# Reordering the passage from the first to the second token group in a fused attention and Fourier-mix kernel

## The chip, the cores and the metric

The kernel runs on one core of a Trainium2 chip. A core has a matrix engine (TensorE, PE in the profile, with its weight loads as PEld), a vector engine (VectorE, DVE), a scalar engine (ScalarE, ACT), a general engine (GpSimd, POOL), a queue engine (SyncE, SP) that issues most transfers, and 16 DMA engines. The metric is the device time in microseconds of one execution; lower is better.

## The reference

Inputs `q`, `k`, `v` have shape (8, 8, 576, 64): batch, heads, tokens, head size. Attention runs within chunks of 64 tokens. Its output, seen as (8, 576, 512), goes through a Fourier mixing block with a two-layer network:

```python
scores = scale * np.matmul(q_c, k_c.transpose(0, 1, 2, 4, 3))   # per chunk of 64
attn = softmax(scores); x = attn @ v_c                          # -> (8, 576, 512)
mixed = np.real(np.fft.fft(np.fft.fft(x, axis=1), axis=2))
u = x + mixed
un = (u - mean(u)) / np.sqrt(var(u) + 1e-6)
out = u + np.maximum(un @ w_ch1, 0.0) @ w_ch2                   # (512, 2048), (2048, 512)
```

The two weights arrive as 64-bit floats and are turned into 32-bit ones in the kernel. All arithmetic is float32.

## The kernel before

Tokens are handled in nine groups of up to 512: one for each of the eight batches and one for the tokens left over at the middle of each sequence. For a group, the two products of the network (first weight `w1` in `wa`, "up"; second weight `w2` in `wb`, "down") are the main loop, and everything else is fed in between: the loop `for _ in mlp(g)` counts steps `t` and after each step emits a share of the attention and the Fourier transform of the next batch (`sides`), of the rounding of the weights (`round_next`), and of stores. Each engine executes its instructions in the order in which they were emitted, so this order is the schedule.

Group 0 uses the plain products: `up_first` takes steps 1 to 16 and `down_plain` steps 17 to 32, one for each of 16 blocks `m` of the second weight, with four matmuls a step. Its four PSUM banks `dn` are freed by the output additions of L1249. From group 1 on a scheme of seven smaller products in place of eight is used (`up_halves`, `down_halves`). It needs sums of weight blocks and sums of token blocks:

- `keep1(pair)` forms the sums of the first weight for one of four pairs of blocks, four GpSimd additions (L1069), the results going into the front of `wb` and back into `wa`. `keep1_store(i)` writes the seven blocks of each pair to DRAM (`s1`): three of them are raw quarters of the weight, `a11`, `a12` and `a22` (numbers 0, 4 and 6), and four are sums (2, 1, 3, 5). Group 1 reads the blocks where they are; later groups read them from DRAM.
- `keep2(i)` forms those of the second weight, four GpSimd additions (L1087) with their stores (L1091) for each of four blocks. `keep2_whole` stores its raw blocks. `conv2` is the list of `keep2` steps; three of them are emitted in each step once all weights are rounded.
- `combined(g, q)` forms the token sums of one half of a group (L1024, L1025, L1026 on VectorE), and with `late` the last of them (L1022).

The passage from group 0 to group 1 runs so. The side work of batch 1 ends with its Fourier transform: products `z`, copies into `zr` and `zf` on ScalarE, and three products `mix` (L838), each followed by a ScalarE copy `y` (L843), two VectorE additions (L848, L849), additions to the tiles (L855, on VectorE for the low tile and GpSimd for the high one), and statistics (L702, L703, and L706, L707 on ScalarE). `normed` makes the normalised tile `un` (L992), `turned` transposes it on TensorE (L397) and copies it into `unT` (L1007). When the four tiles of group 1 are turned and the token sums made, `up_halves(1)` starts with the product `pb` of L1289, which reads the second result of `keep1(0)`. The attention of batch 2 begins in the same steps: scores L448 from `qT` and `kT`, which VectorE transposes (L416), softmax, and the value product L498. For a low tile the first token column of `qT` is copied to the end position, on GpSimd (L418, L431) or on ScalarE (L429).

Transposes, mixes and value products share two PSUM buffers of `ps_t`. `sizes[cur]` is the number of side steps of a batch, and `ready_at` the step by which they are to be done; `due` spreads them evenly. The core's SP queue takes the loads of `q`, `k` (L250), `v` (L273) and of the raw weights (L346), the stores of the outputs (L1037, L1046), of `s1` (L1074) and `s2` (L1091, L1099), and the loads of stored blocks (L1155, L1160), in the order of emission.

Of the kernel before, what the change touches and what calls it, by code (L numbers as in the profile page):

```python
# [16 lines left out]
def kernel(  # L17
# [43 lines left out]
    KF = DFF // 128  # L61
# [5 lines left out]
    G = 2 * NM  # L67
# [35 lines left out]
    NO, HF = 7, KF // 2  # L103
# [77 lines left out]
    NG = len(groups)  # L181
# [219 lines left out]
    def att_T(n, which="qk"):  # L401

        if n > first[2]:
            for src, dst, nm in ((qs, qT, "qT"), (ks, kT, "kT")):
                if nm[0] not in which:
                    continue
                a = src.pop(n).rearrange("p j (t b d) -> p j t b d", t=4, b=2)[:, :, :, 0]  # L410
                t = one_p.tile([128, NJ, 2, CH + 1], FP32, tag=nm, name=nm)
                low = kind(n) == LO and nm == "qT"
                to = t[:, :, :, CH:0:-1] if low else t[:, :, :, 0:CH]
                if kind(n) == HI:
                    to = to[:, :, ::-1]
                nc.vector.transpose(out=to.rearrange("p j c (r t) -> p j t c r", t=4), in_=a)  # L416
                if low:
                    nc.gpsimd.tensor_copy(t[:, :, :, 0:1], t[:, :, :, CH:CH + 1])  # L418
                dst[n] = t.rearrange("p j c t -> p (j c) t")
            if n + 1 < NT:  # L420
                load(n + 1, which)
            return
        a = qs.pop(n)
        pt = turn(lambda j: a[:, 2 * j:2 * j + 2, :].rearrange("p h d -> p (h d)"))
        t = one_p.tile([128, 2 * NJ, CH + 1], FP32, tag="qT", name="qT")
        low = kind(n) == LO
        nc.scalar.copy(t[:, :, CH:0:-1] if low else t[:, :, 0:CH], pt.rearrange("p j (c t) -> p (j c) t", c=2))
        if low and n < first[1]:
            nc.scalar.copy(t[:, :, 0:1], t[:, :, CH:CH + 1])  # L429
        elif low:  # L430
            nc.gpsimd.tensor_copy(t[:, :, 0:1], t[:, :, CH:CH + 1])  # L431
        qT[n] = t
        a2 = ks.pop(n)
        pt = turn(lambda j: a2[:, 2 * j:2 * j + 2, :].rearrange("p h d -> p (h d)"))
        t = one_p.tile([128, NJ, 128], FP32, tag="kT", name="kT")
        nc.scalar.copy(t, pt)
        kT[n] = t.rearrange("p j (c t) -> p (j c) t", c=2)
        if first[1] <= n + 1 < NT:
            load(n + 1)
# [530 lines left out]
        yield  # L970


    uns, unTs = {}, {}

    def natural(n):

# [38 lines left out]
    def combined(g, q_, late=False):  # L1015

        unT = unTs[g]
        cl, ch = slice(q_ * 128, (q_ + 1) * 128), slice(256 + q_ * 128, 256 + (q_ + 1) * 128)
        b11, b12, b21, b22 = unT[:, 0:2, cl], unT[:, 0:2, ch], unT[:, 2:4, cl], unT[:, 2:4, ch]
        t1, t2, t4 = (tt_1[o][:, :, cl] if g == 1 else tt[:, o, :, cl] for o in range(3))  # L1020
        if late:
            nc.vector.tensor_tensor(out=t4, in0=b21, in1=t2, op=ALU.subtract)  # L1022
            return
        nc.vector.tensor_tensor(out=t1, in0=b12, in1=b11, op=ALU.subtract)  # L1024
        nc.vector.tensor_tensor(out=t2, in0=b22, in1=t1, op=ALU.subtract)  # L1025
        nc.vector.tensor_tensor(out=b12, in0=b22, in1=b12, op=ALU.subtract)  # L1026
        if g > 1:
            nc.vector.tensor_tensor(out=t4, in0=b21, in1=t2, op=ALU.subtract)
# [39 lines left out]
        ):  # L1068
            nc.gpsimd.tensor_tensor(out=out_, in0=in0, in1=in1, op=op)  # L1069

    def keep1_store(i):
        pair, o = i // NO, (2, 1, 5, 3, 0, 4, 6)[i % NO]
        to = s1[pair, o].rearrange("p (k x) -> p k x", k=2)
        nc.sync.dma_start(out=to, in_=parts1(pair)[o])  # L1074

# [153 lines left out]
    def down_plain(g, h1):  # L1229

        dns = [ps_f.tile([128, 512], FP32, tag="ff", name="dn") for _ in groups[g]]
        for m in range(KF):
            for s, dn in enumerate(dns):
                nc.tensor.matmul(  # L1236
                    out=dn,
                    lhsT=h1[:, m, s * 128:(s + 1) * 128],
                    rhs=w2[:, m, :],
                    start=(m == 0),  # L1240
                    stop=(m == KF - 1),
                )
                if m == KF - 1:
                    n = groups[g][s]
                    if s < G - 1:
                        o = three_p.tile([128, DM], FP32, tag="o", name="o")
                    else:
                        o = one_p.tile([128, 2 * (HM + 1)], FP32, tag="two", name="o")[:, 0:DM]
                    nc.vector.tensor_tensor(out=o, in0=dn, in1=natural(n), op=ALU.add)  # L1249
                    store(n, o)  # L1250
            for j in range(G):
                due = KF - (G - j + 1)
                if m == due - 2:
                    normed(g + 1, j)
                if m == due:
                    turned(g + 1, j)
                    if j >= 2 and g + 1 >= first_of[1]:
                        combined(g + 1, j - 2)
            yield


# [175 lines left out]
    with tc.manual_schedule():  # L1437
# [60 lines left out]
        begin = [0]  # L1498
        for g in range(NG):
            begin.append(begin[-1] + (KF if g < first_of[1] else 2 * HF) + (KF if g < first_of[2] else 2 * NO if g < FEW else NR2 // 2))  # L1500
        ready_at = [begin[g] + (2 * KF - 7 if g < first_of[2] else 2 * HF + 4) for g in range(NG)]
        conv2 = iter([step for i in range(HF // 2) for step in [keep2(i ^ 1)]])

        def chain(gens):
            for gen in gens:
# [5 lines left out]
        for g in range(NG):  # L1511
            for _ in mlp(g):
# [7 lines left out]
                if cur < len(sides):  # L1520
                    t0 = 3 if cur == 0 else ready_at[cur - 1]
                    t1 = ready_at[cur]
                    due = min(sizes[cur], (t - t0) * sizes[cur] // (t1 - t0))
                    while done < due:
                        heavy = next(sides[cur], None) or heavy
                        done += 1
                    if t >= t1:
                        for _ in sides[cur]:
                            pass
                        cur, done = cur + 1, 0  # L1530
                if not heavy:
                    round_next(late if t < KF and t % 4 == 3 else None)
                    if t <= 2 or t < KF and t % 4 == 0 or t >= KF + 3:
                        round_next()
# [7 lines left out]
                if t == begin[1] - 1:  # L1542
                    for _ in conv2:
                        pass
                if begin[1] - 1 <= t < begin[1] + 7 and t % 2:
                    keep1((t - begin[1] + 1) // 2)
                if t == ready_at[NG - 3]:
                    rest_ = make_rest()
# [6 lines left out]
                    slab3.extend(a.rearrange("p (m e) -> p m e", m=4) for a in more)  # L1555
                if begin[FEW] + 2 <= t < begin[FEW] + 2 + NS3:
                    fetch(3)
                if begin[1] < t < begin[1] + KF:
                    for i in range(2):
                        if n_kept < HF // 2 * NO:  # L1560
                            keep1_store(n_kept)
                            n_kept += 1
                if t in (begin[1] + 9, begin[1] + 13, begin[1] + 16):
                    fetch(2)
                if t == begin[1] + KF:
# [51 lines left out]
```

## Time and profile before

| | |
|---|---|
| median of 3 runs | 1074.06 us (1072.5 to 1075.39) |
| profiled execution, its own time | 1074.23 us |
| its span in the profile | 1072.2 us |
| TensorE busy | 1046.3 us, 98% |
| VectorE busy | 610.8 us, 57% |
| GpSimd busy | 406.6 us, 38% |
| ScalarE busy | 315.3 us, 29% |
| moved by DMA | 212.74 MB, 198 GB/s on average |

Busy times are sums of the recorded instructions of one engine. The profile's own time is that of the span and what lies around it. In a timeline a row gives start, duration, engine, line, operation, the tile written and the tiles read, how many records are merged, and in brackets the idle time just before and what ended it. One float32 matmul of the program shows as two records.

### The profile page before, as it was taken

The page shows a single profiled execution, that of the slowest core. Times are in us where ns is not written, and L with a number is a line of the kernel's source. Part 1 is how long each engine was busy: PE and PEld are TensorE (multiplying, and loading weights), DVE is VectorE, ACT ScalarE, POOL GpSimd, SP SyncE. Part 2 cuts the span into 40 slices and gives each one's busy share as a digit, 9 for nine tenths or more (in the row PEclk, how much of TensorE's full clock was granted, in tenths as well). Part 3 has the DMA queues.
Part 4 walks back from the last instruction along what each step waited for, and adds up shares of the span by engine and source line. Part 5 has one row for each costly group of instructions (what it writes and reads, how often), then busy time and mean ns, then how long its engine had stood idle before and what let it go on. Part 6 is the DMA issues. An engine that isn't in the chain of part 4 may idle for free.

```text
span 1072.2 us, 20212 instructions
## 1 busy us (share of the span) xinstructions
PE 1046.3 (98%) x7498; PEld 854.6 (80%) x7498; DVE 610.8 (57%) x1319; ACT 315.3 (29%) x746; POOL 406.6 (38%) x531
## 2 busy tenths in 40 slices
PE   8999989899999999999999999999999999999997
PEld 6645444688888888888888888788888888888886
DVE  4798986684567465664565554745664535433331
ACT  4688563233113411322032312331133103101200
POOL 4310018672415140344134321614161726780281
PEclk9999999999999999999999999999999999999999
DMA  8767565489668546883667266954654559776763
GB/s 176 232 186 218 123 196 189 139 249 312 233 199 232 149 140 198 239 232 119 191 209 231 99 182 195 231 165 163 202 177 116 208 191 350 229 231 199 272 228 106
DMA packets 157759, 212.74 MB, mean 198 GB/s; under 512 B 69308, under 2 KB 103100, under 8 KB 151390
## 3 DMA queue, kind: packets, MB, share of 16 engines
q1 hardware_dynamic: 154012, 208.04, 63.4%
q10 hardware_dynamic: 3330, 2.76, 1.1%
q8 instruction: 60, 0.98, 0.4%
q0 software_dynamic: 320, 0.66, 0.3%
q14 instruction: 37, 0.30, 0.1%
HBM read 177.31 MB, written 34.08 MB: 197 GB/s over the span
## 4 chain that ended last, share of the span: by engine, by line
PE 77%; DVE 8%; DMA 5%; ACT 4%; SPq 3%; issue 2%; POOL 1%; DVEq 0%; ACTq 0%; POOLq 0%
PE pa L1289 19%; PE pb L1341 18%; PE pb L1289 14%; PE pa L1341 13%; PE dn L1405 4%; PE pt L397 2%; PE mix L838 2%; DMA xall<-in_moe_w_ch_dram 1%; SPq L263 1%; PE xp L498 1%; PE z L719 1%; DVE power L378 1%; DMA out_dram<-o 1%; PE sc L448 1%; DMA v<-in_v_dram 1%
## 5 line engine op out<-in xcount | busy, mean ns | idle before, releaser
L1289 PE MATMUL pa<-unT,wa 128*128 128x256 f32 x736 | 175.0, 381 | 2.5 <-DVE wa L1297 2.5
L1289 PEld LDWEIGHTS pa<-unT,wa 128*128 128x128 f32 x736 | 138.3, 190 | 21.8 <-DVE wa L1297 2.7
L1289 PE MATMUL pb<-wa 128*128 128x256 f32 x448 | 106.9, 381 | 0.1
L1341 PE MATMUL pa<-wb,h 128*128 128x256 f32 x448 | 101.5, 380 | 0.0
L1341 PE MATMUL pb<-wb,h 128*128 128x256 f32 x448 | 100.7, 379 | 0.0
L1289 PEld LDWEIGHTS pb<-wa 128*128 128x128 f32 x448 | 84.1, 190 | 12.3 <-DVE h L1299 0.5
L1341 PEld LDWEIGHTS pa<-wb,h 128*128 128x128 f32 x448 | 83.9, 190 | 11.3
L1341 PEld LDWEIGHTS pb<-wb,h 128*128 128x128 f32 x448 | 84.1, 190 | 11.0
L1169 POOL TENSOR_TENSOR h<-h 128x256 f32<-128x256 f32 x56 | 47.7, 860 | 102.3 <-DVE wb L1167 98.2
L555 POOL COPY xall<-xall 1x512 f32<-1x512 f32 x28 | 17.8, 636 | 154.3 <-DVE xall L515 126.9
L1295 DVE TENSOR_TENSOR wa<-pb,wa 128x256 f32<-128x256 f32 x56 | 23.8, 425 | 69.7 <-ACT wa L1294 69.7
L1289 PE MATMUL pb<-unT,wa 128*128 128x256 f32 x256 | 60.5, 379 | 0.0
L1303 ACT ACTIVATE h<-pa 128x256 f32<-128x256 f32 x64 | 24.6, 384 | 114.1 <-PE pa L1289 113.6
L1236 PE MATMUL dn<-wb,h 128*128 128x512 f32 x128 | 57.5, 597 | 0.0
L1294 ACT COPY wa<-pa 128x256 f32<-128x256 f32 x56 | 20.9, 372 | 123.5 <-PE pa L1289 80.6
L1289 PEld LDWEIGHTS pb<-unT,wa 128*128 128x128 f32 x256 | 48.6, 190 | 6.6
L1289 PE MATMUL pa<-wa 128*128 128x256 f32 x224 | 53.9, 383 | 0.0
L1309 ACT ACTIVATE h<-h 128x512 f32<-128x512 f32 x64 | 39.6, 629 | 45.0 <-DVE h L1308 44.8
L1341 PE MATMUL pb<-wb,yall 128*128 128x256 f32 x224 | 51.2, 381 | 0.0
L1341 PE MATMUL pa<-wb,yall 128*128 128x256 f32 x224 | 50.6, 379 | 0.3 <-DMA wb<-s 0.3
L1341 PE MATMUL pb<-wb 128*128 128x256 f32 x224 | 50.7, 379 | 0.0
L1195 PE MATMUL up<-unT,wa 128*128 128x512 f32 x108 | 49.4, 598 | 0.0
(299 smaller groups left out, 1976.1 us busy)
## 6 DMA issues: line engine op xcount, KB each, us to landing
wb<-s SPq DMA_DIRECT2D x49, 1024.0 KB
wa<-s SPq DMA_DIRECT2D x196, 256.0 KB
xall<-in_moe_w_ch_dram SPq DMA_DIRECT2D x22, 512.0 KB
q<-in_q_dram SPq DMA_DIRECT2D x96, 112.0 KB
k<-in_k_dram SPq DMA_DIRECT2D x96, 112.0 KB
wb<-s SPq DMA_DIRECT2D x16, 512.0 KB
v<-in_v_dram SPq DMA_DIRECT2D x124, 64.0 KB
s<-part SPq DMA_DIRECT2D x30, 256.0 KB
```

Of the source, the lines that this page charges most:

```text
L397: nc.tensor.transpose(pt[:, j, :], src(j), ident)
L838: nc.tensor.matmul(out=mix[:, cols], lhsT=zt[:, T], rhs=tab, start=(T == 0), stop=(T == 3), skip_group_check=True,)
L1169: nc.gpsimd.tensor_tensor(out=h1[:, m, hi], in0=h1[:, m, lo], in1=h1[:, m, hi], op=ALU.subtract)
L1195: nc.tensor.matmul(out=up, lhsT=w1[:, kk, m * 128:(m + 1) * 128], rhs=unT[:, kk], start=(kk == 0), stop=(kk == KD - 1), skip_group_check=True,
L1236: nc.tensor.matmul(out=dn, lhsT=h1[:, m, s * 128:(s + 1) * 128], rhs=w2[:, m, :], start=(m == 0), stop=(m == KF - 1),)
L1289: nc.tensor.matmul(out=dst, lhsT=w[:, kk, r], rhs=rhs[o][:, kk], start=(o in (0, 1) and kk == 0), stop=(kk == 1), skip_group_check=True,)
L1294: nc.scalar.copy(a, dst)
L1295: nc.vector.tensor_tensor(out=b, in0=pbs[r][:, 0], in1=a, op=ALU.add)
L1303: nc.scalar.activation(out=h1[:, m, lo], in_=dst, func=ACTF.Relu)
L1309: nc.scalar.activation(out=h1[:, HF + m], in_=h1[:, HF + m], func=ACTF.Relu)
L1341: nc.tensor.matmul(out=dst, lhsT=lhs[:, m], rhs=w[:, m], start=(o in (0, 2) and m == 0), stop=(m == HF - 1), skip_group_check=True,)
L1405: nc.tensor.matmul(out=dst, lhsT=lhs[:, m], rhs=w[:, m], start=(fresh and not half and m == 0), stop=(m == 3), skip_group_check=True,)
```

## The change

Seven edits, all in the emission order, and one copy on another engine:

- The side steps of batch 1 are spread by `late_due`: the last transform step and the three mixes come at steps 23, 25, 26 and 27 instead of 23, 24, 25 and 25. `ready_at[0]` moves from 25 to 27; batch 2's side steps start two steps later.
- `normed` of group 1's tiles is emitted at `m` = 10, 10, 12, 12 instead of 9, 10, 11, 12; `turned` at 12, 13, 14, 14 instead of 11, 12, 13, 14.
- The token sums are collected in `joined` and emitted after the side step of the same step, both halves at step 31, behind the transpose of batch 2's next `k` tile.
- `keep1(0)` is put into `conv2` after the second `keep2`, ahead of the last two, instead of at step 31 behind them all.
- The twelve raw quarters of the first weight are stored at steps 17 to 20 and 24 to 31.
- The sixteen sums of the first weight are stored one a step from step 32 on; before, all 28 blocks were stored two a step from step 33.
- The token column of batch 2's first tile is copied on ScalarE.

```diff
-        if low and n < first[1]:
+        if low and (n < first[1] or n == first[2]):
             nc.scalar.copy(t[:, :, 0:1], t[:, :, CH:CH + 1])
...
-    uns, unTs = {}, {}
+    uns, unTs, joined = {}, {}, []
...
-    def keep1_store(i):
-        pair, o = i // NO, (2, 1, 5, 3, 0, 4, 6)[i % NO]
+    def keep1_store(pair, o):
         to = s1[pair, o].rearrange("p (k x) -> p k x", k=2)
...
             for j in range(G):
-                due = KF - (G - j + 1)
-                if m == due - 2:
+                if m == (10, 10, 12, 12)[j]:
                     normed(g + 1, j)
-                if m == due:
+                if m == (12, 13, 14, 14)[j]:
                     turned(g + 1, j)
                     if j >= 2 and g + 1 >= first_of[1]:
-                        combined(g + 1, j - 2)
+                        joined.append((g + 1, j - 2))
...
-        ready_at = [begin[g] + (2 * KF - 7 if g < first_of[2] else 2 * HF + 4) for g in range(NG)]
-        conv2 = iter([step for i in range(HF // 2) for step in [keep2(i ^ 1)]])
+        ready_at = [begin[g] + (2 * KF - 5 if g < first_of[2] else 2 * HF + 4) for g in range(NG)]
+        late_due = {ready_at[0] - 4 + i: sizes[0] - x for i, x in enumerate((3, 3, 2, 1, 0))}
+
+        def first_sums():
+            keep1(0)
+            yield
+
+        conv2 = iter([keep2(1), keep2(0), first_sums(), keep2(3), keep2(2)])
...
                     due = min(sizes[cur], (t - t0) * sizes[cur] // (t1 - t0))
+                    if cur == 0:
+                        due = late_due.get(t, (t - t0) * sizes[cur] // (t1 - 2 - t0))
...
+                while joined:
+                    combined(*joined.pop(0))
                 if not heavy:
...
-                if begin[1] - 1 <= t < begin[1] + 7 and t % 2:
+                if begin[1] < t < begin[1] + 7 and t % 2:
                     keep1((t - begin[1] + 1) // 2)
...
-                if begin[1] < t < begin[1] + KF:
-                    for i in range(2):
-                        if n_kept < HF // 2 * NO:
-                            keep1_store(n_kept)
-                            n_kept += 1
+                if KF < t <= KF + 4 or KF + 8 <= t < KF + 16:
+                    keep1_store(n_kept // 3, (0, 4, 6)[n_kept % 3])
+                    n_kept += 1
+                if begin[1] <= t < begin[1] + KF:
+                    keep1_store((t - begin[1]) // 4, (2, 1, 3, 5)[(t - begin[1]) % 4])
```

## The prediction, made before the changed kernel was run

> **What bounds the kernel now.** I read the page first: the busy time of each engine and the row of PE slices.
>
> ```profile
> PE 1046.3 (98%) x7498; PEld 854.6 (80%) x7498; DVE 610.8 (57%) x1319; ACT 315.3 (29%) x746; POOL 406.6 (38%) x531
> PE   8999989899999999999999999999999999999997
> ```
>
> TensorE has work 98% of the span, so 26 us of idle is all that a rearrangement can win. The slices that are not full lie at the start (nothing there changes) and around 134 to 190 us, where group 0's down product ends and group 1 is prepared. Next the waits of PE from 140 to 235 us (waiter, line, what ended the wait, us, times, longest):
>
> ```profile
> PE pb L1289 <- POOL wb L1069: 2.4, 1, 2.4
> PE mix L838 <- DVE y L849: 2.1, 1, 2.1
> PE mix L838 <- ACT zr L785: 1.8, 1, 1.8
> PE pt L397 <- ACT un L992: 1.4, 1, 1.4
> PE sc L448 <- DVE kT L416: 0.7, 1, 0.7
> PE pb L1289 <- DVE h L1308: 0.6, 1, 0.6
> PE xp L498 <- ACT unT L1007: 0.4, 1, 0.4
> PE pb L1289 <- DVE h L1299: 0.3, 1, 0.3
> ```
>
> That is 9.7 us. Up to 192.78 us, where group 1's first product starts, five waits make 8.14 (1.84 + 2.06 + 1.42 + 0.41 + 2.41); behind it lie 1.54, and in the stretch from 240 to 330 us a 0.25 for a transfer. After that PE waits 2.5 more in all, so what is won here should reach the end. The timelines give the distances:
>
> ```profile
> 150.36 0.49 PE L838 MATMUL mix<-ce,zr 128*128 128x129 f32 x2 [1.84 <-ACT zr L785]
> ...
> 159.50 7.03 PE L1236 MATMUL dn<-wb,h 128*128 128x512 f32 x16
> ...
> 192.78 1.99 PE L1289 MATMUL pb<-xall,wb 128*128 128x256 f32 x8 [2.41 <-POOL wb L1069]
> ```
>
> Sixteen `dn` records are two steps of the down product, 6.97 us from 159.50 to the next row at 166.47: one step is 3.48 us. A mix is 1.21 (150.36 to 151.57). One step put between a producer and its reader covers 3.48 us of lateness.
>
> ```profile
> 181.70 0.61 DVE L1024 TENSOR_TENSOR xall<-unT 128x256 f32<-128x256 f32 x1 [8.07 <-ACT unT L1007]
> 182.35 1.37 DVE L1025 TENSOR_TENSOR xall<-unT,xall 128x256 f32<-128x256 f32 x1
> 183.64 1.48 DVE L1026 TENSOR_TENSOR unT<-unT 128x256 f32<-128x256 f32 x1
> ...
> 188.39 0.42 DVE L1026 TENSOR_TENSOR unT<-unT 128x256 f32<-128x256 f32 x1
> ```
>
> The token sums take 0.42 us when GpSimd rests (it did from 186.2 to 190.0) and up to 1.48 while it works through its sums L1087.
>
> **What the Trainium skill says.** "SBUF — State Buffer", section "Who interferes with whom": a VectorE instruction with two SBUF inputs and a GpSimd instruction that reads SBUF exclude each other for the whole instruction. The trace agrees: 0.42 against 1.37 and 1.48 us. "DMA: Bandwidth & Descriptors", section "Issuing engines are not separate DMA queues": a transfer issued elsewhere or earlier still shares the same 16 engines. The trace shows the result only: from 150 to 155 us the DMA share is 0.92, from 155 to 160 it is 0.01.
>
> **The change part by part.** Times below are on the clock of the profile before.
>
> *Transform tail spread.* No instruction is added. The z products end at 144.8 as before; two steps instead of one plus a wait follow, to 151.8, and `zr` is ready at 150.4: the 1.84 goes. Mixes start at 151.8, 156.5 and 161.2 with a step between each. The third needs the first one's PSUM buffer, free when L849 of the rest tile ends. VectorE now does the last weight's three operations first (0.66 + 0.69 + 0.69 from 157.4), so L849 ends at about 160.3: the 2.06 goes, by 0.9 us.
>
> *Normalising tile 0 ahead of tile 1's mix.* On ScalarE the rest tile's rstd stands before tile 0's copy. Rest: add, stats, aggregate 1.73 to 162.0; rstd 0.5 and copy 0.5 to 163.1; L848 and L849 0.9 to 164.0; GpSimd's L855 1.72; stats 0.9 to 166.7; rstd, shift, un 0.5 + 0.5 + 0.8 to 168.6. PE asks for it after two steps from 162.4, at 169.3: the 1.42 goes, with 0.7 to spare. But then ScalarE is the late one: second un 1.3, copy of mix 0.5, L848 and L849 0.9, L855 1.7, stats 0.9, rstd 0.5 bring 174.6; unT copy 0.6, two un of 1.3, unT copy 0.6, exponential 0.6 bring 179.0; the last two unT copies end at 179.6 and 180.2. Turns 2 and 3 now stand together and there are two PSUM buffers, so turn 3 waits until 178.4 instead of starting at 178.1, and the turn of `ex` until 179.6: a new wait of about 1.2 in place of the 0.41. Last step to 183.6, xp and sc 1.1: PE is ready at 184.7.
>
> *First pair's sums ahead on GpSimd.* Four L1069 of 1.27 us move in front of the last eight L1087, to about 173.2 (when L855 of tile 1 ends); the second, which the first product reads, ends at 175.7, so the 2.41 goes. Queued behind them: eight L1087, the token-column copies L418, the stores of those sums on SP, and the k load that SP has behind these stores. GpSimd then runs without a pause to 173.2 + 12 x 1.27 = 188.4.
>
> *Token sums behind k's turn.* Six sums stand after the k transpose (free long before, at 177.4) and cannot start before the unT copy at 179.6. Now GpSimd is busy all through. Not seen as such, so two bounds: all free, 6 x 0.42 = 2.5, end 182.2; all blocked, 0.61 + 5 x 1.42 (the mean of the two rows above) = 7.7, end 187.4. I take blocked, because the eight L1087 lie exactly there. VectorE does the output adds next (L1249, 0.62 each), and the first frees the PSUM bank that the first product needs: 188.0. So the first product starts at 188.0 instead of 192.78: **4.8 us** won; with free sums it would be PE's own 184.7, 8.1 won.
>
> *Stores one stage sooner.* Twelve of 256 KB leave steps 33 to 38 and go to steps 17 to 20 and 24 to 31, and the other sixteen run at one a step. On SP the first four stand between the last weight loads. VectorE waited 0.47 and 0.59 us for those loads at 140.07 and 143.26, so 256 KB ahead at the measured 200 to 300 GB/s can cost the rounding 0 to 2 us; later tasks cover most, I take 0.3. The other eight fall where the DMA share is 0.01 to 0.47. In group 1's up stage SP gains 12 x 0.6 us of issuing, and the block load that PE waited 0.25 for is issued earlier.
>
> *Column copy to ScalarE* (0.2 us): ends long before its reader; nothing either way beyond 0.2.
>
> *Behind the first product.* Of the 1.8 us of waits there I expect 0.5 less: the block wait and part of the rest go, but the k load now comes behind sums ending at 188.4 to 190, and its score is wanted at 199.4. Bounds: 1.8 won, 2 lost.
>
> Sum: 4.8 - 0.3 + 0.5 = 5.0 us off the profiled execution's 1074.23 (span 1072.2 and 2.0 around it), 1069.2; that run lies 0.2 above the median of the runs shown, 1074.06, so 1069.0.
>
> **The rivals.** (1) *All waits go*: GpSimd happens to rest while the token sums run. Against it, its backlog to 188.4. It gives 8.1 to 9.9 us, 1064.2 to 1066. Chance 0.12. (2) *The gain is eaten*: the ScalarE chain runs 2 us later because of the stores, and the score waits 2 more for k; 4.8 - 2 - 2 leaves about 1, and 1071 to 1077 covers its neighbours. For it: two chains with under 1 us to spare. Against it: no transfer was late by more than 0.7 us for PE. Chance 0.17. (3) *Slower*: the queue of SP. Behind the last four stores of L1087's sums, now after 190, stand k, eight output stores, v and q. A k load took 7.00 us to land in the chain of waits; if it lands after about 204.5 instead of the 198.3 that the transpose (1.1) needs, PE and VectorE, both in order, lose over 6 us, and the next k load follows late too: 1078. Chance 0.11. (4) *That the change does little of what it says*: the k transpose is early anyway, so the token sums' new place gains nothing by itself; that is in my sum already.
>
> **How the numbers follow.** The forecast and its neighbours from 3.2 to 8 us won have 0.60. About 0.3% (3.2 us) is what a measurement of this kernel can tell from no change. Faster: 0.60 + 0.12 = 0.72; same 0.17; slower 0.11. The range runs from 1065.0, near the full gain, to 1074.5, which takes in most of the eaten gain; above it lie some 0.13, below it 0.05.
>
> **What would show it.** Right: no PE wait for zr L785, y L849 or wb L1069; mixes a step apart; L1024 to L1026 in one block of six, most near 1.4 us, just before the output adds, and the first product then waiting for VectorE; PE waits of under a microsecond at the third and fourth turns. Wrong: the token sums at 0.42 (then rival 1), a wait of score for kT of over 2 us (rivals 2 and 3), or un L992 ending after PE asks for it.

## The result, and the profile after

The changed kernel takes 1077.42 us (median of 13 runs, 1074.24 to 1082.57), the kernel before, run beside it, 1074.27 (1071.92 to 1076.74). The ratio is 1.0033, 95% interval 1.0019 to 1.0046: slower by about 3.5 us, where 1069.0 was forecast. The profiled execution took 1076.62 us, its span is 1074.6.

The page of the changed kernel, engine busy time and the row of PE slices:

```profile
PE 1046.8 (97%) x7498; PEld 855.5 (80%) x7498; DVE 609.5 (57%) x1319; ACT 315.2 (29%) x746; POOL 408.7 (38%) x531
PE   8999998799999999999999999999999999999997
```

The busy time is what it was. The sixth and seventh slices changed from 8 and 9 to 9 and 8, and the eighth, 188 to 215 us, fell from 8 to 7: that is not the stretch that the change rearranges, but the one behind it. The waits of TensorE from 140 to 235 us say which (waiter, what ended the wait, us in total, times, longest):

```profile
PE pb L1287 <- DVE xall L1293: 5.9, 1, 5.9
PE sc L448 <- POOL qT L418: 2.9, 1, 2.9
PE pa L1287 <- ACT xall L1292: 2.1, 1, 2.1
PE mix L838 <- DVE y L849: 1.1, 1, 1.1
PE pt L397 <- ACT unT L1007: 0.6, 2, 0.3
```

The waits for `zr`, `un` and GpSimd's `wb` are gone, as forecast. Three of 2.1 to 5.9 us are new. TensorE's timeline has their places:

```profile
187.82 0.69 PE L448 MATMUL sc<-kT,qT 64*64 64x64 f32 x32 [2.89 <-POOL qT L418]
188.44 1.99 PE L1287 MATMUL pb<-xall,wb 128*128 128x256 f32 x8
...
194.24 1.99 PE L1287 MATMUL pa<-xall,wb 128*128 128x256 f32 x8 [2.07 <-ACT xall L1292]
...
216.35 3.75 PE L1287 MATMUL pb<-unT,wa 128*128 128x256 f32 x8 [5.87 <-DVE xall L1293]
```

Group 1's first product starts at 188.44 us, 4.3 earlier than before; the forecast had 188.0. From there to the first product of group 1's down stage (`pa` from `wb` and `h`, at 256.1) it is 67.7 us, where the kernel before needs 59.5 (192.78 to 252.3). So 4.3 us were won and 8.2 lost within 70 us. Note also the 3.75 us of the last row: eight records that elsewhere take 1.89 ran at half speed (the granted clock there is 0.5; its mean over the kernel before was 1.000).

Two queues show where the 5.9 and the 2.1 come from. The chain of waits of the changed kernel (start, us, what), shortened:

```profile
198.34 1.18 DVE kT L416
199.52 0.49 SPq L1037
...
200.05 11.00 DMA out_dram<-o
...
212.45 2.34 DMA q<-in_q_dram
...
214.87 0.06 DVE qT L416
...
215.81 0.41 DVE xall L1293
216.22 0.14 issue
216.35 3.75 PE pb L1287 x8
```

The product waits for a VectorE addition, which stands behind the transposition of the next `q` tile; that waits for its load; and SyncE issues the load only when an output store, 11.00 us on its way, has landed. That last stop is 2.2 us long; the queue comes to the load late as well, which the experiments below take apart. Why SyncE has to wait for that store, the profile doesn't say. The 2.1 us is the same on ScalarE's own queue: a copy behind four output stores.

```profile
189.23 4.54 ACTq L1046 DMA_DIRECT2D out_dram<-o  x4
193.81 0.65 ACT L1292 COPY xall<-pa 128x256 f32<-128x256 f32 x2 [12.32 <-DMA out_dram<-o]
```

### The profile page after: what moved, and what is told of

Read it like the earlier page. It is cut to its first block, busy times and chain, and to the rows that moved or that the text cites. A ratio compares the mean times of both kernels' runs of the same rounds, so it can differ in the third digit from the quotient of the medians.

```text
span 1074.6 us, 20210 instructions
## 1 busy us (share of the span) xinstructions
PE 1046.8 (97%) x7498; PEld 855.5 (80%) x7498; DVE 609.5 (57%) x1319; ACT 315.2 (29%) x746; POOL 408.7 (38%) x531
## 4 chain that ended last, share of the span: by engine, by line
PE 82%; DMA 6%; DVE 4%; ACT 3%; SPq 3%; issue 1%; POOL 1%; DVEq 0%; POOLq 0%; ACTq 0%
PE pa L1287 20%; PE pb L1339 18%; PE pb L1287 15%; PE pa L1339 14%; PE dn L1403 4%; PE pt L397 2%; DMA xall<-in_moe_w_ch_dram 2%; PE up L1194 2%; PE mix L838 2%; PE xp L498 1%; PE z L719 1%; SPq L263 1%; DMA out_dram<-o 1%; DMA v<-in_v_dram 1%; PE sc L448 1%
## 5 line engine op out<-in xcount | busy, mean ns | idle before, releaser
L1235 PE MATMUL dn<-wb,h 128*128 128x512 f32 x128 | 57.3, 596 | 0.0
```

What stands on the lines that cost most here:

```text
L1235: nc.tensor.matmul(out=dn, lhsT=h1[:, m, s * 128:(s + 1) * 128], rhs=w2[:, m, :], start=(m == 0), stop=(m == KF - 1),)
```

## The experiments

Each kernel was timed in five rounds against the kernel before on the same chip; each ratio is to the latter. "The start" is that of group 1's first product, "the up stage" the time from there to the first product of its down stage, both in the profiled execution. The profiles are shifted against each other before the passage begins: GpSimd's first second-stage sum (L1087 in the kernel before, L1086 in the changed one) starts between 154.17 us (e3) and 157.69 us (e4). Where two starts are compared closely they are counted from that sum. For the changed kernel and e16 (below):

```profile
155.70 1.39 POOL L1086 TENSOR_TENSOR xall<-wb 128x512 f32<-128x512 f32 x1 [29.60 <-DMA s<-wb]
```

```profile
156.53 1.39 POOL L1086 TENSOR_TENSOR xall<-wb 128x512 f32<-128x512 f32 x1 [29.85 <-DMA s<-wb]
...
188.63 1.99 PE L1287 MATMUL pb<-xall,wb 128*128 128x256 f32 x8 [2.41 <-POOL wb L1069]
```

So the changed kernel starts group 1 after 32.7 us, e16 after 32.1, and the kernel before (155.46 and 192.78) after 37.3.

### First theory: the load behind the output stores

Batch 2's side steps start two steps later, so that the `q` load, which was issued at 189.86 us ahead of the output stores, now comes behind them. Moving the stores should free it. e1 stores the first group's tiles one a step, from the third step of the next stage on:

```diff
-                    store(n, o)
+                    outs.append((n, o))
...
+                if begin[1] + 2 <= t and outs:
+                    store(*outs.pop(0))
```

e2 lets batch 2 start at the old step, e3 puts the weight stores back, and e4 fills the long wait to keep the clock up.

```diff
e2: -                    t0 = 3 if cur == 0 else ready_at[cur - 1]
    +                    t0 = 3 if cur == 0 else ready_at[cur - 1] - 2 * (cur == 1)
e3: all 28 keep1_store calls two a step from step 33, as in the kernel before
e4: +                if g == 1 and pair == 1 and turn_ == 3:
    +                    for _ in range(12):
    +                        nc.tensor.matmul(out=filler[:, 0:NQ], lhsT=ident, rhs=warm[:, 0:NQ], start=True, stop=True)
```

Expected of e1: 

> The changed kernel, with the output stores of group 0 emitted one tile a step at steps 34 to 37 instead of all at step 32. Queue theory (the q load of batch 2's third tile stands on SP behind the output stores and waits for them, VectorE waits for q, TensorE for VectorE): the 9.07 us wait of qT L416 for q and the 5.87 us wait of pb for DVE fall below 1 us each, the half-speed clock behind them goes (1.9 us), and the 2.07 us wait for ScalarE goes too since its queue no longer waits on output stores at 189 us. Sum 8 to 10 us below the changed kernel: 1067 to 1070, ratio to the kernel before 0.994 to 0.996. Port theory (GpSimd's longer backlog and the shared port hold the first group's VectorE work back): VectorE is late anyway, at most 2 us are won, ratio 1.001 to 1.003. Traffic theory (the moved weight stores fill the DMA engines): no gain, and the q load is as late as before, ratio 1.003.

Of e2: 

> The changed kernel, with batch 2's side steps starting from step 25 as in the kernel before; the spread transform tail, the early first sums, the token sums' place and the stores stay. Its q load is emitted at step 31 again, ahead of the output stores. Queue theory: the wait for q goes as in the run with later outputs, 7 to 9 us below the changed kernel, ratio 0.994 to 0.997; the ScalarE wait of 2 us may stay. Port theory: VectorE gets two more transposes among the blocked token sums, so no gain or a loss, ratio 1.003 to 1.006. Traffic theory: ratio 1.003.

Of e3: 

> The changed kernel, with all 28 stores of the first weight's blocks at two a step from step 33, as before; all else as changed. Traffic theory: the loss of 3 us goes and the gain at the first product shows, 5 to 8 us below the changed kernel, ratio 0.995 to 0.998. Queue theory: the q load still stands behind the output stores, with fewer stores ahead of these, so it lands at most 3 us sooner; 0 to 3 us won at the first passage, and the q and k loads that follow have two stores each ahead of them, so part of that is lost again: ratio 1.000 to 1.004.

Of e4: 

> The changed kernel, with 12 matmuls of 128x289 whose result nobody reads put in front of the product pb that waits 5.87 us (some 5.9 us of TensorE work at full clock). Clock theory: after the idle time the granted clock is half for about 4 us and costs 1.9 us; with the filler the clock stays at 1.0, pb takes 1.89 us for its eight records instead of 3.75 and the total falls by 1 to 2 us: ratio 1.001 to 1.002. If the wait is the whole loss and the clock costs nothing: no change, ratio 1.003. If the filler itself outlasts the wait in most executions: ratio up to 1.005.

e1: 1073.46 us, 1.0004 (0.9994 to 1.0014), not the 1067 to 1070 of the queue theory. The 5.9 and 2.1 are gone, but the wait comes again one tile later, at 222 us, behind a `q` load issued at 215.38, and again with half speed after it:

```profile
222.03 3.78 PE L1287 MATMUL pa<-unT,wa 128*128 128x256 f32 x8 [3.22 <-DVE h L1303]
```

e2: 1086.76, 1.0127 (1.0114 to 1.014). No wait for a `q` load is left, and the time is far worse. In the old place the attention steps come before the spread, later end of the transform is done:

```profile
PE pt L397 <- ACT ex L474: 6.0, 1, 6.0
PE sc L448 <- DVE kT L416: 5.6, 1, 5.6
PE pb L1287 <- DVE o L1248: 4.9, 1, 4.9
```

So the later start belongs to the spread tail and can't be taken out alone. e3: 1074.94, 1.0017 (1.0005 to 1.0029); `q` is issued at 204.91 instead of 211.11 and the wait for it falls to 2.8. e4: 1076.76, 1.0035 (1.0023 to 1.0048). The filler keeps full speed,

```profile
212.09 6.00 PE L1281 MATMUL filler<-warm,ident 128*128 128x289 f32 x24
218.18 1.97 PE L1291 MATMUL pb<-unT,wa 128*128 128x256 f32 x8
```

and it delays nothing: this profile is 2.0 us late from the first sum on, and the VectorE addition that the product waits for starts at 217.63 in place of 215.81. So the product takes 1.97 us instead of 3.75, and the up stage is 66.0 us instead of 67.7. The time doesn't show it: 1.0035 against 1.0033, each with an interval of 0.0012 to 0.0014 to either side, or 1.3 to 1.5 us. That the clock alone would have brought the time back is excluded; whether it is worth 1 or 2 us isn't decided.

### The two other waits, and the later start alone

e5 puts the column copy of the first batch-2 tile with a VectorE transposition on ScalarE, e6 issues all twelve output stores of group 0 from GpSimd's queue, e7 does both. e8 is the kernel before with only the later start.

```diff
e5: -                    nc.gpsimd.tensor_copy(t[:, :, :, 0:1], t[:, :, :, CH:CH + 1])
    +                    (nc.scalar.copy if n == first[2] + 1 else nc.gpsimd.tensor_copy)(t[:, :, :, 0:1], ...)
e6: +        sp, act = (nc.gpsimd, nc.gpsimd) if n in groups[0] else (nc.sync, nc.scalar)
    (store uses sp and act)
e8: -        ready_at = [begin[g] + (2 * KF - 7 if ...
    +        ready_at = [begin[g] + (2 * KF - 5 if ...
    -                    due = min(sizes[cur], (t - t0) * sizes[cur] // (t1 - t0))
    +                    due = min(sizes[cur], (t - t0) * sizes[cur] // (t1 - 2 * (cur == 0) - t0))
```

Expected of e5: 

> The changed kernel with one edit: the 128x8 token-column copy of the first batch-2 tile behind the turned one runs on ScalarE instead of GpSimd, where it stands behind seven of the eight second-stage sums and starts 11 us after the transposition that it reads. Theory A (that copy is one of the two places that eat the gain): the 2.89 us wait of TensorE for GpSimd's column copy at 187 us goes, nothing takes its place, the first pass-2 product starts near 185.5 instead of 188.4, and the time falls by 2 to 3 us, to about 1074.5. Theory B (later work is held by the transfers, not by TensorE): the first product is as early, but the wait for the q load at about 215 us grows from 5.9 to about 8.8 us, because that load is issued behind the output stores whenever these finish, and the time stays within 0.8 us of the changed kernel's 1076 to 1077.

Of e6: 

> The changed kernel with one edit: the twelve output stores of the first token group are issued from GpSimd's DMA queue, which stands idle from 190 to 196 us, instead of SyncE's and ScalarE's. Theory A (the order in the queues): SyncE reaches the q load some 6 to 8 us sooner, and ScalarE isn't held by its four stores; the waits of 5.9 us (DVE's tensor behind the q transposition) and 2.1 us (ScalarE's) go, and with the first the stretch at half clock; time 1069 to 1071, 6 to 8 us below the changed kernel. Theory B (the traffic: stores on the way slow every load, whatever queue issued them): q lands at about the same time, the wait stays over 4 us, time within 1 us of the changed kernel. Theory C: as in the run with the stores spread, the wait moves to a later tile, and 3 to 4 us are won, 1073.

Of e7: 

> Both edits: the token-column copy on ScalarE and the first group's output stores on GpSimd's queue. If the two places add up (theory A for both): 1067 to 1069, below both kernels. If the transfers alone set the end: the same as the run with the output stores moved alone.

Of e8: 

> The kernel before with one part of the change: batch 2's side steps start two steps later (its first group's tail stays where it was, at the old steps). Theory A (the later start by itself puts the q load behind the output stores): TensorE gets a wait of 4 us or more for a DVE tensor behind the q transposition between 205 and 225 us, SyncE issues that q load after 205 us instead of at 190, and the time rises by 2 to 5 us, to 1076 to 1079. Theory B (the later start costs nothing by itself; only with the weight stores and the full GpSimd queue of the changed kernel): within 1 us of the kernel before, 1073 to 1075.

e5: 1077.26, 1.0035 (1.0023 to 1.0046), nothing won. The wait for the copy goes and another takes its place: the first product needs a PSUM bank that VectorE frees behind its token sums, and starts 32.8 us after the first sum (32.7 in the changed kernel).

```profile
189.43 1.97 PE L1287 MATMUL pb<-xall,wb 128*128 128x256 f32 x8 [3.01 <-DVE o L1248]
```

e6: 1075.91, 1.0019 (1.0004 to 1.0034), and e7: 1076.04, 1.0031 (1.0018 to 1.0043). Theory A of e6 named the right queue, but twelve stores at once stop GpSimd as they stopped SyncE. Its queue in e7:

```profile
194.39 1.38 POOL L1038 DMA_DIRECT2D out_dram<-o  x2
199.52 1.04 POOL L1047 DMA_DIRECT2D out_dram<-o  x2 [3.75 <-DMA out_dram<-o]
202.21 0.98 POOL L1047 DMA_DIRECT2D out_dram<-o  x2 [1.65 <-DMA out_dram<-o]
```

The `k` load is late as well (in e6 its issue takes 7.47 us), and a score on TensorE waits 3.9 (e6) and 4.6 us (e7) for GpSimd at 207 us. e8: 1077.57, 1.0038 (1.0026 to 1.005), as theory A had it: TensorE waits 5.1 us for L1295 behind the `q` load, whose four parts are issued from 209.22 on. Up to here the later start looked like the whole cause.

### One part of the change at a time

e9 and e10 are the kernel before with the first sums ahead alone, and with the weight stores alone (the sums' stores one step later than in the change, since their sums are at the old place). e11 joins e1 and e6, e12 joins e1 and e3.

Expected of e9: 

> The kernel before with one part of the change: the first pair's four weight sums are issued ahead of the last four second-stage sums on GpSimd; batch 2 starts where it did. Theory A (the 4.8 us priced for the sums ahead is really there, and the loss comes only from batch 2's later start): the 2.4 us wait for GpSimd's sum goes, no wait over 2.5 us comes, the q load stays ahead of the output stores (issued near 190 us), and the time falls by 2.4 to 4.8 us, to 1069 to 1071. Theory B (the sums ahead make GpSimd late for batch 2's column copy, which at the old steps is needed about 178 us): a wait of TensorE for GpSimd's column copy or for DVE behind the shared port comes instead, over 2.8 us, and the time is 1073 to 1077.

Of e10: 

> The kernel before with one part of the change: the stores of the first weight, the twelve raw quarters one stage sooner and the sixteen sums one a step. Theory A (the weight stores harm only by standing in front of a late q load, which this kernel doesn't have): 1073 to 1074, within 1 us of the kernel before. Theory B (they lengthen the queue and the flights by themselves): the k load behind the output stores is issued 3 us or more later than the 202 us of before, a wait of TensorE over 1.5 us between 195 and 225 us is new, and the time rises by 1.5 to 3 us.

Of e11: 

> The changed kernel with the first group's output stores both spread (one token tile a step, from the third step of the next stage on) and issued from GpSimd's queue. Theory A (what held the loads is the place of the stores in SyncE's and ScalarE's queues, and the earlier run with GpSimd's queue lost only because all twelve at once kept GpSimd from its sums and from the column copy until 203 us): no wait of TensorE over 1.5 us between 190 and 240 us, time 1069 to 1071. Theory B (the slow stores on the way hold the loads whatever the queue): a wait over 3 us for a q or k load stays, time 1073 to 1076.

Of e12: 

> The changed kernel with two edits at once that each won some time: the first group's output stores one tile a step later, on the queues as they were, and the weight stores at their old steps. Theory A (both shorten the same queue of SyncE, and the q and k loads then land before they are needed): the wait of 3.2 us that was left with the outputs later goes, 1069.5 to 1071.5. Theory B (the output stores hold the same queue a tile later whatever stands in front): a wait over 2.5 us stays in 205 to 230 us, and the time is that of the outputs spread alone, 1073 to 1074.

e9: 1075.54, 1.0014 (1.0003 to 1.0025). The 2.4 us wait for GpSimd's sum goes and a longer one comes, because second-stage sums, pushed back to 192.1, now run beside all of the token sums, and the second three take 1.37 to 1.48 us each where they took 0.42 before:

```profile
193.98 2.71 PE L1289 MATMUL pb<-xall,wb 128*128 128x256 f32 x8 [3.04 <-DVE o L1249]
```

The start is 0.8 us later than before, counted from the first sum. The part that was to take away the longest of the five waits costs time when it stands alone. e10: 1079.2, 1.0048 (1.0035 to 1.0062), theory B and some 2 us more than its range: the wait for `zr` grows from 1.84 to 3.1, and the `k` load is issued at 207.02 instead of 202.15, after which a score waits 3.1.

e11: 1070.26, 0.9971 (0.9962 to 0.9981). Stores that come singly and leave from a third queue hold no load for long: `q` is issued at 197.50, and the longest wait between 190 and 240 us is 1.4. This beats both kernels and is near the forecast of 1069.0. e12: 1078.41, 1.0043 (1.003 to 1.0055), worse than e1 and e3. Its profiled execution, 1073.6, is the fastest of its 11, and shows waits of TensorE of 2.6 (a score for `kT`) and 2.1 us (a block load); what the slower ones add is not seen.

### Which part carries the gain

e13 makes e11's edit in the kernel before. e14 is e11 with the first sums at their old place, e15 e11 with the weight stores at theirs. e16 is the changed kernel with the first sums back and everything else as changed (in e14 and e16 the stores of the sums come one step later, since they need them), e18 that with the weight stores back too, so the spread tail with the token sums, the later start and ScalarE's column copy alone. e17 is e11 with a filler at the column copy.

```diff
e14, e16, e18:
-        conv2 = iter([keep2(1), keep2(0), first_sums(), keep2(3), keep2(2)])
+        conv2 = iter([keep2(1), keep2(0), keep2(3), keep2(2)])
...
-                if begin[1] < t < begin[1] + 7 and t % 2:
+                if begin[1] - 1 <= t < begin[1] + 7 and t % 2:
                     keep1((t - begin[1] + 1) // 2)
e17: four matmuls of 128x289 into a tile of ps_t ahead of att_S's scores where n == first[2] + 1
```

Expected of e13: 

> The kernel before with the output stores of the first group moved as in the run that won (one tile a step from the third step of the next stage on, from GpSimd's queue), and nothing of the change. Theory A (the change's own gain, set free): in the kernel before, the q load stands ahead of the stores anyway, so nothing much is won: 1073 to 1075. Theory B (the stores' place is the whole gain, the change brings nothing): about 1070, the same as the changed kernel with this edit.

Of e14: 

> The changed kernel with the outputs later on GpSimd's queue, and the first pair's weight sums back at their old place behind the second-stage sums (their stores a step later, as they need them). Theory A (the forecast's term for the sums ahead): the wait of about 2.4 us for GpSimd's sum at the first product is back, the first product starts 2 to 5 us later than in that version, and the time is 1072.5 to 1075. Theory B (the first product is set by DVE's token sums either way, and GpSimd frees the port sooner without the sums ahead): the same time within 1 us, 1069.5 to 1071.

Of e15: 

> The changed kernel with the outputs later on GpSimd's queue, and the weight stores at their old steps. Theory A (the stores one stage sooner serve only to leave the later queue free, and cost nothing once the output stores are gone from it): two stores a step stand again between the loads of the next stage, some load is late by 1 to 3 us, and the time is 1071 to 1074. Theory B (their cost seen before is one of traffic at 170 to 190 us): 1068 to 1070, below the version without this edit.

Of e16: 

> The changed kernel with one edit: the first pair's weight sums back behind the second-stage sums (their stores a step later). The output stores are where the change has them. Theory A (the sums ahead cost 4 us by the late column copy and the half clock after it): the 2.9 us wait for GpSimd's column copy goes, a 2.4 us wait for GpSimd's sum at the first product comes, the wait behind the q load stays: 1072 to 1074. Theory B (the loads behind the output stores set the end whatever comes before): the q wait grows by what the start wins, 1076 to 1078.

Of e17: 

> The changed kernel with the outputs later on GpSimd's queue, and four matmuls of 128x289 into an unused tile ahead of the scores that wait for GpSimd's column copy (about 2 us of filler in a wait of 2.9 us). Theory A (most of the cost of the first sums is the half clock after that wait): no stretch under full clock between 185 and 200 us, and the time 2 to 4 us below that version, 1066.5 to 1068.5. Theory B (the clock there costs nothing that lasts, as with the longer filler at 212 us): within 1 us of it, 1069.5 to 1071.

Of e18: 

> The kernel before with the spread tail of the transform, the token sums moved and the later start of batch 2, and neither the first sums ahead nor the weight stores moved. Theory A (the tail wins 3 us at the first product and the later start then loses as much and more behind the output stores): first product at 189 to 190 us, a wait of 3 us or more for a DVE tensor behind the q load at 205 to 220 us, 1073 to 1076. Theory B (it is the moved weight stores in front that make the q load late enough to matter): no such wait over 2.5 us, 1069 to 1071.

e13: 1072.97, 0.9987 (0.9976 to 0.9998): the stores' place is worth little without the change. e15: 1070.39, 0.9973 (0.9964 to 0.9982), no different from e11 and in neither theory's range.

e14: 1066.22, 0.9942 (0.9929 to 0.9955), the best of all, 3.1 us below e11 in the ratios and 4.0 in the medians. Neither theory had this. Its waits from 140 to 235 us:

```profile
PE pb L1288 <- POOL wb L1070: 2.4, 1, 2.4
PE mix L838 <- DVE y L849: 1.6, 1, 1.6
PE pt L397 <- ACT unT L1007: 0.6, 2, 0.3
PE mix L838 <- ACT zr L785: 0.3, 1, 0.3
```

The wait that the sums ahead were to remove is back, and still the start, 189.50, comes 32.1 us after the first sum (157.39), where e11's comes after 32.9 (188.76 and 155.86). No wait follows it, and its up stage takes 57.3 us (e11: 60.3).

e17: 1076.17, 1.002 (1.0013 to 1.0027), a failure of the experiment: the filler needed a `ps_t` buffer that VectorE freed only at 191.7, so it made a wait of 6.1 us instead of filling one. It tells nothing of the clock. e16: 1071.45, 0.9975 (0.9964 to 0.9985), just below the range of theory A and with the three waits as it had them; but the half clock that theory A blames does not follow the column copy's wait in the changed kernel, whose first product runs in 1.99 us. e18: 1070.89, 0.9968 (0.9956 to 0.9979), theory B: no wait in the up stage is over 0.2.

e18, e16, e3 and the changed kernel make a square, all with the spread tail and the later start:

| first sums, weight stores | `q` load issued, us | start, us | the same from the first sum | up stage, us | waits in it | lost in it to half speed | ratio to before |
|---|---|---|---|---|---|---|---|
| old, old (e18) | 200.0 | 187.22 | 32.1 | 59.5 | 0.2 | 1.7 | 0.9968 |
| old, sooner (e16) | 204.6 | 188.63 | 32.1 | 62.5 | 3.4 | 1.5 | 0.9975 |
| ahead, old (e3) | 204.9 | 187.32 | 33.2 | 64.3 | 2.8 | 4.0 | 1.0017 |
| ahead, sooner (changed) | 211.1 | 188.44 | 32.7 | 67.7 | 7.9 | 2.1 | 1.0033 |

The time lost to half speed is TensorE's busy time multiplied by the missing part of the granted clock. Waits and half speed explain the up stage: without them 57.4 to 57.7 us are left in all four.

The sums ahead make the start no earlier but later, by 1.1 and 0.6 us, and lengthen the up stage by 4.8 and 5.1. That is 5.8 to 5.9 us together; the ratios have 5.3 and 6.2. Of the longer up stage 2.6 and 4.5 us are waits, and the rest is half speed, which comes in part by chance (see the last section). The weight stores alone make a difference of 0.7 and 1.7 us in the ratios, inside their intervals. So the later start, which in e8 looked like the cause, does no harm with the tail that it was made for; the first sums do.

Where the waits come from is in SyncE's queue. The changed kernel:

```profile
181.83 3.13 SPq L1090 DMA_DIRECT2D s<-xall  x4
...
187.75 2.83 SPq L1090 DMA_DIRECT2D s<-yall  x4
...
191.82 3.84 SPq L250 DMA_DIRECT2D k<-in_k_dram  x4
...
203.39 4.25 SPq L273 DMA_DIRECT2D v<-in_v_dram  x4
...
211.11 1.77 SPq L250 DMA_DIRECT2D q<-in_q_dram  x4
```

And e16, with the sums at the old place:

```profile
177.53 2.80 SPq L1090 DMA_DIRECT2D s<-xall  x4
...
183.78 2.33 SPq L1090 DMA_DIRECT2D s<-yall  x4
...
186.78 4.48 SPq L250 DMA_DIRECT2D k<-in_k_dram  x4
...
199.45 4.24 SPq L273 DMA_DIRECT2D v<-in_v_dram  x4
...
204.61 3.80 SPq L250 DMA_DIRECT2D q<-in_q_dram  x4
```

The four additions put first make eight second-stage sums 4.2 us later on GpSimd (the first of them at 179.10 instead of 174.88). Their stores wait in SyncE's queue, and everything behind them, k, outputs, v and q, is 3.7 to 6.5 us later, although none of it reads those sums. With the output stores out of this queue the sums ahead still cost time (e11 against e14): 0.8 us at the start and 3.0 in the up stage, of which 1.4 is a wait at 221 us and 1.4 half speed, which in e11 follows the wait of 2.9 us for GpSimd's late column copy.

## Why the prediction was wrong, point by point

- **Transform tail and normalising ahead: right, and worth more than was credited.** With the token sums' new place, from which no run separates them, they carry the whole gain at the start: e16 and e18, without the sums ahead, start 5.2 us earlier than the kernel before, counted from the first sum. The waits for `zr` and `un` went; that for `y`, given as gone by 0.9 us, stayed at 1.1. The first of the last weight's three operations (L377) takes 1.75 us in its new place and not the 0.66 of the working, and TensorE is free for the third mix at 160.4 and not at 161.2. The waits for turns and `ex` are 0.6 in place of the 1.2.
- **Token sums all blocked: right.** They take 0.48 and then 1.37 to 1.48 us, end at 187.7 (forecast 187.4), and the start is at 188.44 (188.0). In part that is luck: the changed kernel's first product was to wait for VectorE, but it follows TensorE's wait for the column copy; VectorE's first output addition ends at about 188.25 (187.63 and a quarter of 2.47), and only e5 shows the product waiting for it. "SBUF — State Buffer" of the Trainium skill, section "Who interferes with whom", agrees with this trace: beside GpSimd's sums, which run from 174.05 to 190.2, all but the first of these additions take over three times the 0.42 us that they took before while GpSimd rested:

```profile
180.19 0.48 DVE L1024 TENSOR_TENSOR xall<-unT 128x256 f32<-128x256 f32 x1 [1.88 <-ACT unT L1007]
180.71 1.38 DVE L1025 TENSOR_TENSOR xall<-unT,xall 128x256 f32<-128x256 f32 x1
182.01 1.48 DVE L1026 TENSOR_TENSOR unT<-unT 128x256 f32<-128x256 f32 x1
```

- **First pair's sums ahead: the step that failed, in its credit and in its price.** It took the 2.41 us wait as won. But GpSimd's sum and VectorE's blocked token sums reach the first product at about the same time: take one away and the other holds it (e9, without the spread tail: 3.04 us for VectorE; e16, with it: 2.41 for GpSimd, and a start 0.6 us earlier than with the sums ahead). In e16 the sum ends at 188.58 and the first output addition at about 188.0. The working had both numbers, a sum at 175.7 and an output addition at 188.0, but did not ask when the sum would have come at its old place once the tail was spread.
- **"Queued behind them", the price of the same step: named, and put at nothing.** The list has "eight L1087, the token-column copies L418, the stores of those sums on SP, and the k load". This is what turned a gain into a loss: putting the sums back wins 5 to 6 us (e16 against the changed kernel, e18 against e3). The column copy starts at 187.37, 10 us behind its transposition, and TensorE waits 2.9 for it, though e5 shows that VectorE would have held the product as long. The stores cost more (4.5 us of further waits against e16): the list ends at k, where the queue goes on to the outputs, v and the next q, issued at 211.11 instead of 204.61. They are not all of it, since with the output stores out of the queue the sums ahead still lose 3.1 us (e11 against e14).
- **Behind the first product: 0.5 less expected, 8.2 more measured**, outside the bound of 2. Of it some 5 come with the first sums and 3 with the weight stores (67.7, 62.5 and 59.5 us in the square), half speed included, which the working did not have.
- **Stores one stage sooner, 0.3 us: too small.** The first second-stage sum starts at 156.6 us in the mean of the twelve profiles that have these stores sooner, at 155.4 in the eight that have them at the old steps: so about 1.3 us are lost before the passage begins. "The other eight fall where the DMA share is 0.01 to 0.47" is misread: the profile before has 0.78, 0.92 and 0.83 in the three stretches from 175 to 190 us, and in the changed kernel the last three raw quarters are issued at 185.01, 190.63 and 195.70, among the sums' stores, q, k and the outputs. e10 loses 5.2 us, part of it on ScalarE, whose `zr` is 1.4 later. Under the spread tail 0.7 to 1.7 remain. The wait for a block load is 1.1 in e18, 2.1 in e12 and 2.8 in e15, which have the stores at their old steps (e3 has none), and none in the changed kernel, e11, e14 and e16.
- **Rival 3** had the right queue and, nearly, the time (1078), but the wrong load and the wrong point: `k` came early enough, while the next `q` did not. It had 0.11, since its price was put on one transfer and not on all that follow in the queue.

What stays open: how much of the half speed is chance, since each kernel has one profile (e3's is 2.0 us faster than its median), and so how the 5 to 6 us divide between late loads and clock. Beyond 330 us e14 shows no wait, e11 two that make 1.9; what removes them was not tried, nor was e11 with the column copy on ScalarE.

## What to carry to other kernels

When work is moved ahead on one engine, follow what is moved back: its own readers first, then the stores that wait for it in an in-order queue, and then every load behind these stores, to the last one that is needed within the delay. Before crediting a removed wait, ask what the same instruction waits for next; where two inputs of a product are late, mending one of them alone wins nothing. Output stores are read by nobody in the kernel and should not stand ahead of loads: here, spread and on a queue with no load to issue, they won 6.7 us in the changed kernel (e11) and 1.4 in the kernel before (e13).

## What was not expected of the hardware

- A wait of TensorE of 2 to 3 us can be followed by half speed, in which eight matmul records take 3.4 to 3.8 us instead of 1.9. In the twenty profiles it came, from 140 us on, after 6 of 11 waits of 2.0 to 2.2 us, 3 of 7 of 2.4 to 2.5, the one of 2.6, 8 of 10 of 2.8 to 2.9, 3 of 5 of 3.0 to 3.1, and after all 11 of 3.2 us and more. TensorE's timeline in e18 and in e14:

```profile
187.22 3.68 PE L1287 MATMUL pb<-xall,wb 128*128 128x256 f32 x8 [2.41 <-POOL wb L1069]
```

```profile
189.50 1.99 PE L1288 MATMUL pb<-xall,wb 128*128 128x256 f32 x8 [2.42 <-POOL wb L1070]
```

  "TensorE: Matmul & The Clock Gate" of the Trainium skill, section "What's actually happening", puts half rate behind an idle window of about 3.4 us that runs freely. The free running agrees with a result that differs from run to run; waits of 2.0 to 2.4 us that suffice are shorter than the page's window. The half speed added 1.3 (e10, from 160 us on) to 3.0 us (e15, sixteen records in 6.68 us instead of 3.69) to such a wait, and may be part of the scatter of the changed kernel's times; that was not tried.
- Output stores are slow to land: the one in the chain above took 11.00 us, the last part of the `q` load behind it 2.34; issued from GpSimd, those of 128 KB took 8.8 us and those of 64 KB 8.0 (medians of four and eight, e11). "DMA: Bandwidth & Descriptors", section "Issuing engines are not separate DMA queues", says that another issuing engine saves only the time of issuing. Here it saved more, since the issuing queue also stops for earlier stores: from 185 to 240 us SyncE waits 7.1 us for output stores in e1, where they are spread, and not at all in e11, where the same stores leave from GpSimd, and e11 is 3.5 us faster (1.0004 and 0.9971).
